# Windowed attention: the output transposed in PE's transpose mode into bf16 PSUM, copied by VectorE and kept by window

## Chip, cores, metric

One core of one Trainium2 chip. The metric is the device time of one execution in microseconds (us), median of two to seven runs of a kernel. The runs of the kernel before went from 5329 to 5375 us over the chips of this study, so each variant is judged against runs of the kernel before of the same call. All runs quoted here are of the state "fast".

## The reference, cut to what matters

```python
x0 = x + depthwise_conv3x3(x)                 # x: 1 x 511 x 511 x 192, bf16
h  = layernorm(x0)                            # over the 192 channels
hw = windows(h)                               # 7 x 7 windows: 5329 windows of 49 tokens
q, k, v = split(hw @ w_qkv)                   # 4 heads of 48
out = softmax(q k^T * 48**-0.5) v
return x0 + unwindow(out @ w_o)
```

## The kernel before

Windows are worked in 42 blocks of 128. A block has 16 steps, one for each chunk of 8 windows (392 tokens). The stages of several chunks overlap: in iteration g, A makes Q, K and V of chunk g, B the scores and the exponential of chunk g-1, D the weighted sum and its normalisation of chunk g-2, and E transposes the output of chunk g-3 into `OT`. Once a block there also run: the projection of the previous block (iteration 3), the convolution of the next block (iterations 7 to 10), the layer-norm statistics of the next block (iterations 11 to 15), with two "inverse roots" (1/std for 28 and then 21 tokens, each a chain of 15 small VectorE operations), and, at the start of the next block, the transposes of the normalised input (`hT`).

```python
PS = _Rot([psum.tile([128, 1024], F32, name=f"ps{i}") for i in range(4)])   # four PSUM buffers, in turn
OT = big.tile([128, 2, S * BLK], BF, name="OT")                            # S = 49 tokens, BLK = 128 windows
...
def build_D(blk, g):                       # diagonal matrices of 1/std: the transposes normalise as well
    nc.gpsimd.tensor_tensor(out=D[:], in0=ident_broadcast, in1=rstd[:, s0 : s0 + NDG]_broadcast, op=ALU.mult)
...
def transposes(blk):                       # 7 groups of 7 tokens, two halves of the channels each
    matmul(ps, lhsT=xc[:, s0 + ss, kt * KT : (kt + 1) * KT], rhs=D[:, ss, :])
    if kt == 0 or g % 2 == 0: nc.scalar.copy(out=hT..., in_=ps)
    else:                     nc.vector.tensor_copy(out=hT..., in_=ps)     # 3 of 14
...
def proj(blk):
    matmul(ps, lhsT=OT[0:KT, kt, (s0 + ss) * BLK : (s0 + ss + 1) * BLK], rhs=Wo[kt][0:KT, :])
...
def stage_E(g):
    for kt in range(2):
        for jj in range(4):
            nc.tensor.matmul(
                ps[0:KT, kt * 512 + jj * 2 * S : kt * 512 + (jj + 1) * 2 * S],
                lhsT=o_[:, jj, kt * KT : (kt + 1) * KT], rhs=idv, start=True, stop=True)
    nc.scalar.copy(
        out=OT[0:KT].rearrange("p k (s w) -> p k s w", w=BLK)[:, :, :, ck * CH : (ck + 1) * CH],
        in_=two_bank(ps, TOK)[0:KT].rearrange("p k (w s) -> p k s w", s=S))
...
if ck >= cend:                             # iterations 11 to 15
    stats_part(nb, sa, sb)                 # 10 rows of bn_stats on VectorE
    if sa < 28 <= sb:                      # the first inverse root, 28 rows
        stats_fin(nb, 0, 28);  build_D of groups 0 to 3   (GpSimd)
    if ck == NCH - 1:                      # the second inverse root, 21 rows
        stats_fin(nb, 28, 49); build_D of groups 4 to 6
```

`dve_help` decides who copies the second half of Q, K and V: VectorE in iterations 0 to 10, ScalarE in 11 to 15. A scheduler orders the instructions of each engine, so the written order is not quite the built one. The code above is shortened; "..." marks cuts, and names such as `ident_broadcast` stand for longer access patterns.

## Time and profile before

Median 5343.16 us (2 runs, 5342.79 to 5343.53). Mean length of the steps of a block in the profiled run, from the first QK matmul of one chunk to that of the next, in us:

| step | what lies in it | us |
|---|---|---|
| 0, 1 | plain | 4.80, 4.80 |
| 2 | projection | 14.34 |
| 3 to 5 | plain | 4.70, 4.78, 4.80 |
| 6, 7 | plain, then convolution and its wait for a load | 4.77, 20.11 |
| 8 to 10 | convolution and its end, granted clock 0.53 to 0.63 | 11.46, 7.32, 6.00 |
| 11 to 14 | statistics | 4.82, 4.73, 5.13, 4.99 |
| 15 | second inverse root, D, transposes | 15.87 |

The sum is 123.4 us a block. This is the group of the transposes (L346) in the kernel before: count, busy us, mean ns of one, then PE's idle time before them in us and what ended it; it will be compared later:

```profile
L346 PE MATMUL ps<-D,XC 128*96 128x128 bf16 x4116 | 338.4, 240 | 164.5 <-DVE hT L357 77.6 <-POOL D L327 35.8 <-ACT hT L355 26.2
```

In the whole run the transposes waited 36 us for GpSimd's diagonal matrices D (L327), and 78 us for VectorE's copies of earlier transposes (hT, L357), which in this kernel stand behind the second inverse root in VectorE's queue.

### The profile page before, as it was taken

The numbers are of one execution on the slowest core, as the hardware profiler recorded it, in microseconds if no ns is written. First come the engines' busy times: TensorE is split into PE (matmuls) and PEld (weight loads), VectorE is DVE, ScalarE is ACT, GpSimd is POOL, SyncE is SP. The second block draws the span as 40 slices with busy tenths as digits, with TensorE's granted clock in tenths as the row PEclk, the third lists the DMA queues.
The fourth block names the chain that finished last, engine by engine and source line by source line (L and its number), as shares of the span: only waits on it lengthen the run. The fifth ranks groups of instructions, "written<-read, shape, count | busy, mean of one in ns | idle before, by whom it ended". The sixth has DMA issues, their size and how long they took to land.

```text
span 5337.2 us, 148265 instructions
## 1 busy us (share of the span) xinstructions
PE 4490.1 (84%) x65427; PEld 3661.5 (69%) x65427; DVE 3816.7 (72%) x6912; ACT 2744.5 (51%) x3385; POOL 758.0 (14%) x833
## 2 busy tenths in 40 slices
PE   2788888888888888888988888888888888888887
PEld 1666676667776676677776777767666776677776
DVE  6776777767776777777677777777777777767776
ACT  1554555545555555555555455555555555545555
POOL 1111111111111111111111111111111111111120
PEclk9887888887778887888788877788888888877888
DMA  6554445554455555554455544455555445544431
GB/s 67 51 75 70 68 71 80 82 73 68 68 68 70 71 72 74 71 74 71 68 73 91 75 68 68 68 72 72 74 72 72 73 70 78 85 74 67 68 48 32
DMA packets 512613, 375.27 MB, mean 70 GB/s; under 512 B 453129, under 2 KB 453321, under 8 KB 511958
## 3 DMA queue, kind: packets, MB, share of 16 engines
q1 hardware_dynamic: 480918, 265.08, 38.1%
q0 software_dynamic: 30592, 100.32, 10.6%
q8 instruction: 514, 8.42, 0.7%
q14 instruction: 141, 1.16, 0.1%
q10 hardware_dynamic: 448, 0.30, 0.0%
HBM read 265.31 MB, written 100.27 MB: 68 GB/s over the span
## 4 chain that ended last, share of the span: by engine, by line
PE 44%; DVE 16%; ACT 14%; DMA 12%; SPq 9%; issue 4%; POOL 1%; DVEq 0%; ACTq 0%; POOLq 0%
PE ps L412 12%; PE ps L282 8%; SPq L396 7%; DMA out_dram<-XC 7%; PE ps L369 6%; DMA XC<-in_x_dram 5%; PE ps L453 5%; PE ps L532 4%; DVE kT L424 4%; ACT hT L355 4%; DVE Qb L422 3%; PE ps L431 2%; DVE XC L284 2%; PE ps L560 2%; ACT kT L426 2%
## 5 line engine op out<-in xcount | busy, mean ns | idle before, releaser
L412 PE MATMUL ps<-hT,Wqk 96*128 96x392 bf16 x5336 | 1233.5, 380 | 76.7 <-DVE XC L284 62.2
L478 ACT ACTIVATE PT<-ps 128x784 bf16<-128x784 f32 x667 | 552.7, 829 | 1095.3 <-PE ps L453 1080.3
L421 ACT CAST Qb<-ps 64x784 bf16<-64x784 f32 x667 | 555.3, 833 | 657.5 <-PE ps L412 655.7
L412 PEld LDWEIGHTS <-Wqk 96*128 96x128 bf16 x5336 | 529.4, 108 | 486.1 <-issue 252.5
L284 DVE TENSOR_TENSOR XC<-ps,XC 128x980 bf16<-128x980 f32 x378 | 437.9, 1176 | 503.0 <-PE ps L282 247.2
L282 PE MATMUL ps<-T,XP 81*128 81x49 bf16 x8064 | 744.0, 264 | 55.5 <-DMA XP<-in_x_dram 55.5
L567 ACT CAST OT<-ps 96x784 bf16<-96x784 f32 x667 | 541.0, 811 | 456.0 <-PE ps L560 452.4
L282 PEld LDWEIGHTS <-XP 81*128 81x128 bf16 x8064 | 733.9, 220 | 57.6 <-issue 55.5
L431 PE MATMUL ps<-Wv,hT 96*128 96x192 bf16 x5336 | 663.5, 277 | 16.4 <-DVE On L544 9.0
L532 PE MATMUL ps<-V,PT 49*64 49x49 bf16 x21344 | 542.5, 195 | 159.1 <-DVE Qb L422 81.2
L431 PEld LDWEIGHTS <-hT 96*128 96x128 bf16 x5336 | 548.8, 111 | 180.0 <-issue 91.6
L544 DVE TENSOR_TENSOR On<-ps,rs 128x768 bf16<-128x768 f32 x667 | 634.6, 951 | 16.0
L532 PEld LDWEIGHTS <-PT 49*64 49x64 bf16 x21344 | 466.2, 116 | 260.4 <-issue 217.7
L327 POOL TENSOR_TENSOR D<-ident,rstd 128x896 bf16<-128x896 bf16 x294 | 486.2, 1681 | 1074.8 <-DVE rstd L320 1053.3
L424 DVE CAST kT<-ps 128x784 bf16<-128x784 f32 x462 | 450.0, 974 | 219.2 <-PE ps L412 209.1
L304 DVE BATCH_NORM_STATS2 bnst<-XC 128x6 f32<-128x192 bf16 x2058 | 600.5, 343 | 0.2
L453 PE MATMUL ps<-Qb,kT 128*64 128x98 bf16 x10672 | 408.0, 225 | 180.7 <-DVE Qb L422 132.2
L422 DVE CAST Qb<-ps 64x784 bf16<-64x784 f32 x462 | 451.6, 978 | 110.6 <-ACT Qb L421 100.1
L355 ACT CAST hT<-ps 96x896 bf16<-96x896 f32 x462 | 452.4, 1109 | 135.9 <-PE ps L346 134.9
L560 PE MATMUL ps<-ident,On 128*96 128x98 bf16 x5336 | 412.1, 226 | 114.4 <-DVE kT L424 110.9
L453 PEld LDWEIGHTS <-kT 128*64 128x64 bf16 x10672 | 341.5, 121 | 231.5 <-issue 131.7
L108 POOL DMA_DIRECT2D XC<-in_x_dram x386 | 216.0, 560 | 1865.9 <-DVE rs L543 996.3
(73 smaller groups left out, 4396.2 us busy)
## 6 DMA issues: line engine op xcount, KB each, us to landing
XC<-in_x_dram POOLq DMA_DIRECT2D x277, 294.0 KB, 7.5
out_dram<-XC SPq DMA_DIRECT2D x277, 294.0 KB
XP<-in_x_dram SPq DMA_DIRECT2D x210, 246.4 KB
XP<-in_x_dram SPq DMA_DIRECT2D x68, 243.0 KB
XC<-in_x_dram POOLq DMA_DIRECT2D x37, 165.4 KB, 7.1
out_dram<-XC SPq DMA_DIRECT2D x37, 165.4 KB
XP<-in_x_dram SPq DMA_DIRECT2D x22, 216.0 KB
XP<-in_x_dram SPq DMA_DIRECT2D x18, 212.6 KB
```

The source lines that it names most:

```text
L282: nc.tensor.matmul(ps[:, col : col + S], lhsT=XP[0:KP, :, c], rhs=T[0:KP, c, :], start=True, stop=True)
L304: nc.vector.bn_stats(out=bnst[:, s, :], in_=xc[:, s, :])
L355: nc.scalar.copy(out=hv[0:KT, kt, :, s0 : s0 + NDG], in_=src)
L412: nc.tensor.matmul(ps[:, ab * 512 : ab * 512 + TOK], lhsT=Wqk[kt][0:KT, which * 2 + ab, :], rhs=hT[0:KT, kt, ck * CH : (ck + 1) * CH, 0:S] ...
L421: nc.scalar.copy(out=dst[0:64, :, :, 0, :], in_=src[0:64])
L422: (nc.vector.tensor_copy if dve_help else nc.scalar.copy)(out=dst[64:128, :, :, 1, :], in_=src[64:128])
L424: nc.vector.tensor_copy(out=dst[:, :, 0:TOK], in_=two_bank(ps, TOK))
L431: nc.tensor.matmul(ps[:, col : col + C], lhsT=hT[0:KT, kt, ck * CH + 2 * jj : ck * CH + 2 * jj + 2, :].rearrange("p w s -> p (w s)"), rhs= ...
L453: nc.tensor.matmul(ps[64 * wp : 64 * wp + 64, col : col + 2 * S], lhsT=k_[:, ab, w * S : w * S + 64], rhs=q_[:, ab, w, :, :].rearrange("p ...
L478: nc.scalar.activation(out=pt[:, 0 : 16 * S].rearrange("p (b n) -> p b n", b=2), in_=two_bank(ps, 8 * S), func=ACTF.Exp, scale=scale,)
L532: nc.tensor.matmul(ps[64 * wp : 64 * wp + 64, col : col + S], lhsT=pt[64 * wp : 64 * wp + S, pc_ : pc_ + 64], rhs=v_[64 * wp : 64 * wp + S ...
L544: nc.vector.tensor_tensor(out=o_[:].rearrange("p (b j) (h d) -> p b (j h) d", b=2, d=DH), in0=ov[:, :, :, 0:DH], in1=r_[:].rearrange("p (b ...
```

## The change

Intent: free ScalarE, which empties PSUM three to six times a step, of one copy; let the transposes write bf16 so that VectorE's copy gets shorter; and keep the output window by window, so that this copy's rows are written one after another. The price is that the projection's weights are then read with a step of 49 elements.

```diff
-        OT = big.tile([128, 2, S * BLK], BF, name="OT")
+        OT = big.tile([128, 2, BLK * S], BF, name="OT")
@@ proj
-                            lhsT=OT[0:KT, kt, (s0 + ss) * BLK : (s0 + ss + 1) * BLK],
+                            lhsT=OT[0:KT, kt, :].rearrange("p (w s) -> p s w", s=S)[:, s0 + ss, :],
@@ stage_E
+            pb = ps[:].bitcast(BF)
...
-                        ps[0:KT, kt * 512 + jj * 2 * S : kt * 512 + (jj + 1) * 2 * S],
+                        pb[0:KT, kt * 1024 + jj * 128 : kt * 1024 + (jj + 1) * 128],
                         lhsT=o_[:, jj, kt * KT : (kt + 1) * KT],
-                        rhs=idv,
+                        rhs=ident[:],
+                        is_transpose=True,
...
-            nc.scalar.copy(
-                out=OT[0:KT].rearrange("p k (s w) -> p k s w", w=BLK)[:, :, :, ck * CH : (ck + 1) * CH],
-                in_=two_bank(ps, TOK)[0:KT].rearrange("p k (w s) -> p k s w", s=S),
+            nc.vector.tensor_copy(
+                out=OT[0:KT, :, ck * TOK : (ck + 1) * TOK].rearrange("p k (w s) -> p k w s", s=S),
+                in_=pb.rearrange("p (k n) -> p k n", k=2)[0:KT, :, 0 : CH * 64].rearrange("p k (w s) -> p k w s", s=64)[:, :, :, 0:S],
             )
```

## The prediction

> **What bounds the kernel now.** I read the shares of the engines first. No engine is full, so the shares only say where to look.
>
> ```profile
> PE 4490.1 (84%) x65427; PEld 3661.5 (69%) x65427; DVE 3816.7 (72%) x6912; ACT 2744.5 (51%) x3385; POOL 758.0 (14%) x833
> ```
>
> ACT, which the change relieves, is the least loaded of the three compute engines, and DVE, which takes the work, is 1.4 times as busy. Next I cut one block of 16 steps (a step is one chunk of 8 windows; there are 42 blocks) out of the middle of the run at the first QK matmul of chosen steps, and asked for the busy time of each engine in five stretches: the projection of the previous block; four plain steps; the convolution; the steps with the layer-norm statistics; the last step with the transposes of the next block. Columns: us, then busy us of PE, weight loads, DVE, ACT, POOL, then the granted clock.
>
> ```profile
> 2659.57:2674.05 14.48, 14.05 (x201) 13.01 (x197) 10.45 (x13) 6.90 (x10) 0.00 (x0) 1.00 0.01 3
> 2674.05:2693.06 19.01, 15.37 (x292) 11.86 (x290) 15.84 (x19) 10.37 (x14) 3.74 (x7) 1.00 0.91 192
> 2693.06:2732.26 39.20, 35.06 (x415) 29.43 (x410) 23.34 (x26) 7.32 (x10) 1.34 (x3) 0.56 0.21 32
> 2732.26:2755.33 23.07, 19.36 (x363) 14.60 (x363) 21.22 (x76) 19.92 (x27) 2.67 (x6) 1.00 0.71 73
> 2755.33:2771.60 16.27, 12.29 (x175) 10.50 (x173) 11.32 (x26) 14.88 (x18) 9.90 (x7) 0.90 0.75 72
> ```
>
> The projection is PE's (14.05 of 14.48). In the statistics DVE has only 1.85 of 23.07 us free. The transposes look like ACT's (14.88 of 16.27). The convolution runs at a clock of 0.56. Then the timeline of the plain step and of the last step:
>
> ```profile
> 2657.44 0.98 DVE L422 CAST Qb<-ps 64x784 bf16<-64x784 f32 x1
> 2658.45 0.96 DVE L438 CAST V<-ps 128x768 bf16<-128x768 f32 x1
> 2659.57 1.53 PE L412 MATMUL ps<-hT,Wqk 96*128 96x392 bf16 x8
> 2659.68 0.26 DVE L543 RECIPROCAL rs<-ps 128x16 f32<-128x16 f32 x1 [0.27 <-PE ps L532]
> 2659.97 0.96 DVE L544 TENSOR_TENSOR On<-ps,rs 128x768 bf16<-128x768 f32 x1
> 2661.21 0.98 DVE L424 CAST kT<-ps 128x784 bf16<-128x784 f32 x1 [0.28 <-PE ps L412]
> ...
> 2763.05 4.97 POOL L327 TENSOR_TENSOR D<-ident,rstd 128x896 bf16<-128x896 bf16 x3 [2.78 <-DVE rstd L320]
> 2764.02 5.16 PE L346 MATMUL ps<-D,XC 128*96 128x128 bf16 x56 [2.27 <-DVE hT L357]
> ```
>
> The plain step is a loop: V's copy frees the PSUM buffer, QK's matmuls follow, then the copies of K, Q and V: 4.77 us from QK to QK. DVE is free in it only for 0.27 + 0.28 us. In the last step the transposes wait for the diagonal matrices D, those wait on POOL, and POOL waits for the last operation of the inverse root on DVE. So ACT's 14.88 us is busy work behind a chain that DVE starts. Last, the convolution's first evacuation waits for data:
>
> ```profile
> DVE XC L284 <- DMA XC<-in_x_dram: 215.9, 34, 10.5
> ```
>
> That is 6.4 us in each of 34 blocks: from the projection through store and load to the convolution runs a DMA chain, beside the plain steps.
>
> [...] the convolution's weights, 192 elements apart, take 220 ns a load where contiguous ones take 98. [...]
>
> ```profile
> L282 PEld LDWEIGHTS <-XP 81*128 81x128 bf16 x8064 | 733.9, 220 | 57.6 <-issue 55.5
> L369 PEld LDWEIGHTS <-OT 96*128 96x128 bf16 x4116 | 360.4, 98 | 27.6 <-issue 26.4 <-ACT OT L567 1.1
> L567 ACT CAST OT<-ps 96x784 bf16<-96x784 f32 x667 | 541.0, 811 | 456.0 <-PE ps L560 452.4
> ```
>
> **The change part by part.**
>
> ACT loses 667 copies x 811 ns = 541 us. Where is that on the path? In the plain steps ACT is half idle: nothing. In the statistics steps it looks like something, as ACT has 19.92 of 23.07. But without the copy Q's first half still cannot be read before QK's matmuls give it, and those come after the transposes of the same step on PE; I follow K's copy, scores, transposes, QK, the two Q copies and K's copy round and get 4.5 us against 4.6 now. So ACT's relief is worth about 0.1 us a step, and PE's longer transposes take it back.
>
> DVE gains 667 copies. [...] The built program of the changed kernel shows where they stand. In the plain step: after V's copy, ahead of the reciprocal. There V, copy, reciprocal, On need 0.03 + 0.57 + 0.03 + 0.29 + 0.96 + 0.03 = 1.91 us before K's copy, which now starts 1.80 after V's end: +0.11 a step. Of the some 6 such steps of a block, those between projection and convolution lie beside the DMA chain and are free; 2 count: 42 x 2 x 0.11 = 9 us.
>
> In the statistics steps: the scheduler also moves the rows, 10 in each of the first steps where there were 11, so the 28 rows that the first inverse root needs are ready a step's end later. From the fourth reciprocal (2750.3 by today's clock) I add 0.2 + 0.35 + 0.95 + 0.2 + 0.6 and ten pairs of one small operation and one row of 0.36: the first inverse root ends near 2755.8, against 2753.6 today. Then the fifth reciprocal, copy, On and nine rows (0.2 + 0.9 + 0.95 + 2.45) end near 2760.4, and the second inverse root follows with two of the hT copies (1.1 each) now in between, its first two operations held up by POOL's first four D as today (1.4 and 1.7 us): it ends near 2766 to 2768, against 2762.97. POOL's three D (4.97), the last transposes and the last copies hang on it rigidly. I take +3.8 us a block, x 41 = 156 us; 1.5 to 5.5 us is what my reading allows.
>
> PE's transposes stream 128 columns where they had 98. Today's spacing at full clock is (520 - 207)/7 = 45 ns for 98 columns (8 in 0.52 us); the hT transposes, 128 columns with weights of the same shape, go at 55 (7 in 0.55 us, of which 0.22 is the last). If PE mode keeps that, +10 ns x 8 a chunk, which counts only where PE bounds: in the convolution's three or four steps at half clock, where it is some 0.2 us each: 42 x 0.6 = 25 us.
>
> The projection's 4116 weight loads now step by 49 elements. The convolution's strided loads go every 90 ns (80 in 7.30 us); the projection's matmuls are 82 apart. If loads overlap the streams as now, 90 replaces 82 at most: 98 x 6 to 8 ns x 42 = 25 to 33 us, on PE's own stretch. I take 25.
>
> Sum: 5343 + 156 + 9 + 25 + 25 = 5558 us.
>
> **The rivals.** (a) Relief of ACT wins: the statistics and transposes drop by up to a copy a step, 6 x 0.8 x 41 = 197 us, to 5150. For it: ACT's 14.88 of 16.27. Against: D and the wait on the inverse root above. (b) [...] each copy costs 0.40 more; the two plain steps +34 us, the statistics +2 us a block = 82 us: 5670. [...] (c) A strided load does not hide under the stream: 90 + 20 to 80 ns a matmul, up to +280 us, to 5800. Against: in the convolution the streams are already under the loads. (d) [...] the clock falls in the plain steps as in the convolution (0.56): steps of 6.6 us in place of 4.8, over +500 us. [...] (e) The DVE delay is swallowed by other slack, as DVE is free 1.85 us in the statistics: then only some +60 to 100 us remain, within 2%.
>
> **Range and chances.** (e) is the main way to land within 2%, and needs the statistics stretch to lose under 1.2 us a block: 0.2. (b), (c), (d) all push up, so the range reaches further up: 5400 to 5740. Faster needs (a), against DVE's order: 0.03. Slower: 0.77.
>
> **What would show it.** DVE's OT copy at about 574 ns and DVE near 4200 us busy; plain steps of 4.9 us; the projection stretch 0.6 us longer; POOL's last three D of a block 3 to 5 us later after the convolution; the granted clock still 1.00 in the plain steps. I am wrong if the last D come no later, if the plain step shortens, or if strided loads cost far more than 90 ns.

The sum came to 5343 + 156 + 9 + 25 + 25 = 5558 us. The 574 ns for VectorE's bf16 copy enters the sums behind the 9 and the 156 as 0.57 and 0.6 us, and the 0.40 of rival (b) is the 974 ns of K's fp32 copy less it. No run before the change showed it, so read it there as an assumption of mine; the changed kernel's copy then took 560 ns (373.5 us in all), the fp32 copy of run 2 963.

## The result, and the profile after

Median 5525.51 us (2 runs, 5517.59 to 5533.42): slower, ratio 1.0336 with a 95% interval of 1.0295 to 1.0377. A ratio is the mean time of one kernel's fast runs over that of the other's of the same rounds, so it is not quite the ratio of the medians that I quote.

The shares of the engines of the changed kernel:

```profile
PE 4639.7 (84%) x65427; PEld 3773.8 (68%) x65427; DVE 4092.8 (74%) x7579; ACT 2257.2 (41%) x2718; POOL 758.0 (14%) x833
```

ACT lost 487 us of busy time, DVE gained 276, PE 150. The five stretches of a block from the middle of the run, cut at the same steps as in the prediction (us; busy us of PE, weight loads, DVE, ACT, POOL; granted clock; DMA share; GB/s):

```profile
2740.19:2754.78 14.59, 14.27 (x200) 13.20 (x196) 10.76 (x14) 6.99 (x10) 0.00 (x0) 1.00 0.01 2
2754.78:2774.17 19.39, 16.11 (x292) 12.22 (x291) 17.91 (x25) 6.68 (x9) 3.94 (x7) 1.00 0.91 191
2774.17:2813.17 39.00, 35.50 (x409) 29.79 (x408) 24.40 (x29) 4.95 (x6) 1.14 (x2) 0.56 0.23 31
2813.17:2836.43 23.26, 19.61 (x363) 15.00 (x363) 21.50 (x72) 17.08 (x22) 1.00 (x4) 1.00 0.71 74
2836.43:2856.03 19.60, 12.82 (x173) 11.07 (x172) 12.55 (x35) 14.60 (x17) 11.57 (x7) 0.83 0.75 69
```

Four stretches changed by less than 0.4 us. The last grew from 16.27 to 19.60. ACT does about the same amount of work there as before, 14.60 us, in a longer stretch: it waits. Selected lines from the timeline of that last stretch of the changed kernel (start us, us, engine, line, operation, in brackets the idle time before and what ended it):

```profile
2836.73 6.61 POOL L327 TENSOR_TENSOR D<-ident,rstd 128x896 bf16<-128x896 bf16 x4 [22.13 <-DVE rstd L320]
2836.93 0.50 DVE L569 COPY OT<-ps 96x784 bf16<-96x784 bf16 x1
2838.22 2.42 DVE L304 BATCH_NORM_STATS2 bnst<-XC 128x6 f32<-128x192 bf16 x9
2841.67 1.72 DVE L311 TENSOR_TENSOR tmp<-bnst 128x21 f32<-128x21 f32 x1
2843.73 1.08 DVE L357 CAST hT<-ps 96x896 bf16<-96x896 f32 x1
2845.89 1.08 DVE L357 CAST hT<-ps 96x896 bf16<-96x896 f32 x1
2847.79 4.97 POOL L327 TENSOR_TENSOR D<-ident,rstd 128x896 bf16<-128x896 bf16 x3 [4.45 <-DVE rstd L320]
2849.52 4.94 PE L346 MATMUL ps<-D,XC 128*96 128x128 bf16 x42 [4.10 <-POOL D L327]
```

The first four D begin 23.56 us after the stretch of statistics began (2813.17), where it was 21.40 before (2753.66 less 2732.26); the last three 34.62 us after, where it was 30.79. PE's transposes now wait for D, as their group says for the whole run:

```profile
L346 PE MATMUL ps<-D,XC 128*96 128x128 bf16 x4116 | 383.6, 257 | 285.4 <-POOL D L327 234.6 <-ACT hT L355 22.5 <-DVE hT L357 19.3
```

The wait for D grew by 199 us, but PE's idle time before the transposes by 121 only: two of the three hT copies now stand inside the second inverse root, so that less time is spent waiting for those.

Over all blocks, the steps' means changed like this (us a block): steps 0 and 1 -0.12; step 2 +0.10; steps 3 to 5 -0.01; 6 and 7 +0.31; 8 to 10 +0.32; 11 to 14 +0.42; 15 +3.67. The sum is 4.69, which times 41 to 42 blocks is the 194 us by which the two profiled spans differ. So nearly four fifths of the loss is in one step of sixteen. These are profiles of one execution each; differences of 0.1 to 0.4 us in steps 7 to 14 also occur between runs that change nothing there (run 4 has +0.25 in step 7).

### The profile page after: what moved, and what is told of

The parts are those of the page before. It is cut to its first block, busy times and chain, and to the rows that moved or that the text cites. A ratio compares the mean times of both kernels' runs of the same rounds, so it can differ in the third digit from the quotient of the medians.

```text
span 5531.4 us, 148053 instructions
## 1 busy us (share of the span) xinstructions
PE 4639.7 (84%) x65427; PEld 3773.8 (68%) x65427; DVE 4092.8 (74%) x7579; ACT 2257.2 (41%) x2718; POOL 758.0 (14%) x833
## 5 line engine op out<-in xcount | busy, mean ns | idle before, releaser
L412 PE MATMUL ps<-hT,Wqk 96*128 96x392 bf16 x5336 | 1249.0, 383 | 70.2 <-DVE XC L284 48.8
L412 PEld LDWEIGHTS <-Wqk 96*128 96x128 bf16 x5336 | 542.3, 109 | 484.9 <-issue 259.7
L346 PE MATMUL ps<-D,XC 128*96 128x128 bf16 x4116 | 383.6, 257 | 285.4 <-POOL D L327 234.6
L346 PEld LDWEIGHTS <-XC 128*96 128x96 bf16 x4116 | 346.5, 153 | 328.9 <-issue 264.2
L561 PE MATMUL ps<-ident,On 128*96 128x128 bf16 x5336 | 487.3, 243 | 95.5 <-DVE kT L424 91.8
L561 PEld LDWEIGHTS <-On 128*96 128x96 bf16 x5336 | 412.0, 139 | 152.6 <-issue 125.8
```

Source lines behind the costliest of these rows:

```text
L346: nc.tensor.matmul(ps[0:KT, ss * 128 : (ss + 1) * 128], lhsT=xc[:, s0 + ss, kt * KT : (kt + 1) * KT], rhs=D[:, ss, :], start=True, stop=True,)
L412: nc.tensor.matmul(ps[:, ab * 512 : ab * 512 + TOK], lhsT=Wqk[kt][0:KT, which * 2 + ab, :], rhs=hT[0:KT, kt, ck * CH : (ck + 1) * CH, 0:S] ...
L561: nc.tensor.matmul(pb[0:KT, kt * 1024 + jj * 128 : kt * 1024 + (jj + 1) * 128], lhsT=o_[:, jj, kt * KT : (kt + 1) * KT], rhs=ident[:], is_ ...
```

## The experiments

The theory: VectorE's copies, with the orders that come with them, delay the two inverse roots, GpSimd's D follow, and the transposes of the last step wait. The rivals: PE's transpose mode, the strided weights, or VectorE's time wherever it stands. To read the runs I took from each trace, in the mean over blocks 1 to 39, when the first and the fifth D begin after the QK of step 10: 23.62 and 33.10 us before, 26.08 and 37.51 in the changed kernel. From the fifth D to the end of step 15 it is 8.47 us before and 8.08 in the changed kernel, so the whole loss of these steps lies before the fifth D: 2.46 us of it before the first D, and 1.96 between the first and the fifth, where two hT copies of 1.08 us now stand. So the lower granted clock of step 15 (0.82, it was 0.91) costs nothing after the fifth D; what that of step 11 (0.83, it was 0.93) costs before it was not separated.

**1. ScalarE copies instead (changed kernel, one thing undone).**

```diff
-            nc.vector.tensor_copy(
+            nc.scalar.copy(
                 out=OT[0:KT, :, ck * TOK : (ck + 1) * TOK].rearrange("p k (w s) -> p k w s", s=S),
```

> The changed kernel with one thing undone: ScalarE instead of VectorE copies the bf16 transposes. Theory (the VectorE queue in front of the inverse root is the cost): the inverse root ends where it did before the change, POOL's last three D come at 30.8 us after the block's statistics begin, not 34.6, and the time is 5343 plus only what PE's longer transposes cost, 5345 to 5385. Rival (PE-mode transposes or strided weights cost most of it): 5450 or more whoever copies. ScalarE's copy of bf16 PSUM about 0.81 us.

Measured 5362.77 us, ratio 1.0024 (0.9981 to 1.0067). First D at 23.56, fifth at 32.98. The loss is gone, and in this build no hT copy stands inside the second inverse root; what PE mode and the layout cost together is not told apart from zero. The copy itself, in the groups of this run (mean ns of one after the comma):

```profile
L569 ACT COPY OT<-ps 96x784 bf16<-96x784 bf16 x667 | 540.4, 810 | 506.5 <-PE ps L561 485.8
```

ScalarE takes 810 ns for bf16 where it took 811 for fp32.

**2. VectorE copies, nothing else (kernel before, one thing done).**

```diff
-            nc.scalar.copy(
+            nc.vector.tensor_copy(
                 out=OT[0:KT].rearrange("p k (s w) -> p k s w", w=BLK)[:, :, :, ck * CH : (ck + 1) * CH],
```

> The kernel before with one thing changed: VectorE makes the attention output's copy, still fp32 and with the old layout. Theory: 784 fp32 elements cost VectorE about 0.97 us against 0.56, and five copies of a block lie ahead of the second inverse root, so some 2 us a block more than the change: 5560 to 5680. Rival (the loss comes from PE mode or the layout): 5343 to 5400.

Measured 5730.89 us, ratio 1.0700 (1.0633 to 1.0767): the expected direction, and more than expected. First D at 29.32, fifth at 41.05. One copy, in the groups of this run, beside that of the changed kernel:

```profile
L567 DVE CAST OT<-ps 96x784 bf16<-96x784 f32 x667 | 642.3, 963 | 138.2 <-PE ps L560 123.6
```

```profile
L569 DVE COPY OT<-ps 96x784 bf16<-96x784 bf16 x667 | 373.5, 560 | 52.2 <-PE ps L561 47.6 <-PE ps L282 2.9 <-ACT PT L478 0.6
```

So the bf16 part of the change is a gain on its own terms: it makes VectorE's copy 0.40 us shorter and with the rest of the change halves the loss. What I had not counted: with 963 ns the other steps grow too (step 2 by 1.19 us, step 6 by 0.91, steps 10 to 14 by 3.5). As in the changed kernel, two hT copies stand inside the second root here.

**3. Split by step (changed kernel).**

```diff
-        def stage_E(g):
+        def stage_E(g, on_act=False):
...
-            nc.vector.tensor_copy(
+            (nc.scalar.copy if on_act else nc.vector.tensor_copy)(
...
-                stage_E(g - LE)
+                stage_E(g - LE, on_act=(fast and ck >= 11))
```

> The changed kernel, but ScalarE copies in the five steps with statistics (steps 11 to 15 of a block) and VectorE in the others. Theory: the last-step loss of 3.7 us a block goes, about 150 us: 5355 to 5400. Rival (the loss is spread over all steps, or is a matter of the clock): the gain is in proportion, 5 of 16 copies of 182 us, so about 5465.

Measured 5421.00 us, ratio 1.0122 (1.0074 to 1.0170), a little above the 5355 to 5400 of the theory and clearly below the 5465 of the rival. Five of sixteen copies moved, 31% of them, and some 60% of the loss went. It is not all: first D at 24.30, fifth at 34.84, so 1.7 us of delay stay. The order of this build shows one reason that I had not foreseen: the scheduler put one hT copy inside the second inverse root here as well, and moved the rows of the statistics. The times tell them apart in part: from the first to the fifth D it is 10.55 us where it was 9.48, so the one hT copy makes 1.07 of the 1.74. The other 0.68 lies before the first D, and how it divides between the moved rows and the copies in the convolution steps was not separated.

**4. The layout alone (kernel before).**

```diff
-                            lhsT=OT[0:KT, kt, (s0 + ss) * BLK : (s0 + ss + 1) * BLK],
+                            lhsT=OT[0:KT, kt, :].rearrange("p (w s) -> p s w", s=S)[:, s0 + ss, :],
...
-                out=OT[0:KT].rearrange("p k (s w) -> p k s w", w=BLK)[:, :, :, ck * CH : (ck + 1) * CH],
-                in_=two_bank(ps, TOK)[0:KT].rearrange("p k (w s) -> p k s w", s=S),
+                out=OT[0:KT, :, ck * TOK : (ck + 1) * TOK],
+                in_=two_bank(ps, TOK)[0:KT],
```

> The kernel before with the layout alone: the copies stay fp32 and on ScalarE, the output is kept by window, so the projection's weight loads step by 49 elements. Theory: a load takes 141 ns in place of 98 but hides under the 192-column stream, matmuls stay 83 ns apart, and the time stays within 0.5% of 5343. Rival of my prediction: up to 8 ns a matmul, 5370. ScalarE's copy with rows written one after another may be a little shorter than 811 ns.

Measured 5345.54 us, ratio 0.9985 (0.9942 to 1.0029). The groups of this run for the projection's weight loads:

```profile
L369 PEld LDWEIGHTS <-OT 96*128 96x128 bf16 x4116 | 409.7, 142 | 22.9 <-issue 21.8 <-ACT OT L567 1.0
```

A load takes 142 ns where it took 98, and it is hidden: in this run's trace, as in the changed kernel's, the starts of the projection's matmuls (those that add the input included) are on average 83.6 ns apart, 83.5 before. ScalarE's copy took 809 ns, as with strided rows.

**5. All hT copies on ScalarE (changed kernel).**

```diff
-                    if kt == 0 or g % 2 == 0:
+                    if fast or kt == 0 or g % 2 == 0:
                         nc.scalar.copy(out=hv[0:KT, kt, :, s0 : s0 + NDG], in_=src)
```

> The changed kernel, with ScalarE making the three hT copies of a block that VectorE makes. In the trace of the changed kernel two of them, 1.08 us each, stand inside the second inverse root. Theory: without them the fifth D of a block comes about 2 us earlier (35.4 us after the QK of step 10 instead of 37.5), of which most reaches the end: 5525 less 41 x 1 to 2 us, 5440 to 5490. Rival (ScalarE with 14 copies then bounds the last step): no gain, 5510 to 5560.

Measured 5494.87 us, ratio 1.0293 (1.0259 to 1.0327), runs of the kernel before at 5343.61. The fifth D came 2.5 us earlier (35.03), as expected, and from the first D to the fifth it is 9.40 us again, as before the change, so the two hT copies do stand in the chain. But against the changed kernel the time fell by only some 23 us by the ratios, 31 by the medians, less than the 35 to 85 expected. As the two kernels were not run in the same call and the intervals of their ratios overlap, even that gain is not clear of noise. In the profiles step 15 gained 1.0 us and step 0 gave 0.46 back: after the fifth D the block now took 9.08 us in place of 8.08, and PE's transposes waited 43 us for ScalarE's hT copies in place of 22. So ScalarE, with 14 hT copies, seems to be the next limit. The rival of this run was half right.

**6 and 7. The same dummy work in two places (kernel before).** A sum over 384 elements of the output, thrown away; five a block, in iterations 3 to 7 or 11 to 15.

```diff
+            if pad:
+                nc.vector.tensor_reduce(out=junk[:], in_=o_[:, 0:2, :].rearrange("p j c -> p (j c)"), op=ALU.add, axis=AX.X)
...
-                stage_E(g - LE)
+                stage_E(g - LE, pad=(fast and 3 <= ck <= 7))        # run 6
+                stage_E(g - LE, pad=(fast and ck >= 11))            # run 7
```

> The kernel before, with a dummy VectorE operation of about 0.5 us (a sum over 384 elements of the attention output, thrown away) in steps 3 to 7 of each block, five a block, some 110 us of VectorE work in all. Theory (work there hides in the plain loop's gaps and beside the DMA chain): within 0.7% of the kernel before, 5343 to 5380. Rival (VectorE time counts wherever it stands): +110 us, 5450.

Measured 5398.99 us, ratio 1.0095 (1.0069 to 1.0121): more than expected, though only half of the VectorE time that was added.

> The kernel before with the same dummy operation, five a block, but in steps 11 to 15, ahead of and between the two inverse roots. Theory: it repeats the change's loss without PE mode, layout or bf16: the first D 2 us later, the fifth 3 to 4.5 us later, the time 5343 + 41 x 2.5 to 4 = 5445 to 5510. Rival (only the copies' PSUM buffers or PE matter): within 1% of before.

Measured 5499.06 us, ratio 1.0282 (1.0247 to 1.0317), as expected. The dummies in the groups of run 6 and of run 7:

```profile
L573 DVE TENSOR_REDUCE junk<-On 128x1 f32<-128x384 bf16 x210 | 116.1, 553 | 7.2
```

```profile
L573 DVE TENSOR_REDUCE junk<-On 128x1 f32<-128x384 bf16 x208 | 111.2, 534 | 0.1
```

The same 111 to 116 us of VectorE work cost 55 us in one place and 155 in the other. In run 7 the fifth D begins at 36.75 (+3.65) and step 15 is 3.17 us longer: the change's loss, without its transpose mode, layout or bf16. The dummies do not make all of it by their own time: in this build, too, the scheduler put two hT copies inside the second root, and 2.04 of the 3.65 us lie between the first and the fifth D. In run 6 no hT copy moved, and the fifth D stays at 33.13. Run 6 is not clean: as built, two of its five dummies stand ahead of the projection, and the scheduler swapped the K and Q copies in every other step; step 2 grew by 0.60 us and step 6 by 1.46, of which step 7, whose convolution waits for a load, gave 0.81 back.

**8. A try to beat both: Q's second half on ScalarE (kernel before).**

```diff
-                    (nc.vector.tensor_copy if dve_help else nc.scalar.copy)(out=dst[64:128, :, :, 1, :], in_=src[64:128])
+                    nc.scalar.copy(out=dst[64:128, :, :, 1, :], in_=src[64:128])
```

> A try to beat both: the kernel before, with the second half of Q copied by ScalarE in every step, which takes 0.98 us out of the VectorE loop of the plain steps (4.77 us) and puts 0.81 on ScalarE, idle there for 2.3 us. Theory: plain steps fall to about 4.0 us, but only the two before the projection and the projection's own step are on the path, as those after it lie beside the DMA chain: 42 x 1.5 to 2.5 us, 5240 to 5290. Rival (the plain steps are bounded by PE and its waits): 5330 to 5350.

Measured 5356.59 us (5317.31 to 5377.26), ratio 1.0032 (0.9997 to 1.0066): a miss. The profile is of the fastest of the four runs, the one of 5317 us. In it the plain steps did fall, from 4.78 to 4.25 us, but most of the gain was given back. Step 6 grew by 0.51 us, step 7 by 1.23, as the convolution's first evacuations waited longer for their load, and steps 11 to 13 by 0.93, at a mean granted clock of 0.77, 0.90 and 0.91 where it had been 0.95, 0.96 and 0.94. The wait, in the list of run 8, beside the 215.9 us in 34 blocks that the prediction quotes:

```profile
DVE XC L284 <- DMA XC<-in_x_dram: 280.8, 37, 11.3
```

**9. No wait for the second inverse root (run 5).**

```diff
-                in1=rstd[:, s0 : s0 + NDG].unsqueeze(2).to_broadcast([128, NDG, 128]),
+                in1=rstd[:, (g % 4) * NDG : (g % 4 + 1) * NDG].unsqueeze(2).to_broadcast([128, NDG, 128]),
...
-                        for gg in range(4):
+                        for gg in range(NG):
                             build_D(nb, gg)
...
-                            for gg in range(4, NG):
-                                build_D(nb, gg)
```

> A wrong result on purpose: the run with all hT copies on ScalarE, but the last three D of a block are built from the first inverse root's values right after the first four, so that no D waits for the second inverse root, which VectorE still computes. Instructions on PE and VectorE stand in the same order as in that run. Theory (the second root is what the last D, the transposes and the block's end wait for): the fifth D comes about 6.7 us after the first (it was 9.4), the last step 1.5 to 3 us shorter, 5495 less 41 x 1.5 to 3 = 5370 to 5435. Rival (the last step is bound by ScalarE's copies or by PE): 5480 to 5500.

Measured 5553.52 us, ratio 1.0374 (1.0318 to 1.0430): slower, against the expectation. (The comparison with the reference passed it although three groups of each block were scaled by other rows' values; it does not see this error.) The fifth D did come 6.6 us after the first, and PE waited 74 us for D in place of 168. But step 15 shrank by 0.3 us only, and step 0 grew by 1.1. Selected lines from the timeline of a last step of this run show two reasons:

```profile
2874.43 11.54 POOL L327 TENSOR_TENSOR D<-ident,rstd 128x896 bf16<-128x896 bf16 x7 [24.65 <-DVE rstd L320]
2879.37 1.72 DVE L311 TENSOR_TENSOR tmp<-bnst 128x21 f32<-128x21 f32 x1
2879.44 12.65 ACT L355 CAST hT<-ps 96x896 bf16<-96x896 f32 x13
2881.01 1.70 DVE L310 TENSOR_TENSOR tmp<-tmp 128x21 f32<-128x21 f32 x1
2882.64 1.72 DVE L312 TENSOR_SCALAR tmp<-tmp 128x21 f32<-128x21 f32 x1
2884.39 1.61 DVE L313 SCALAR_TENSOR_TENSOR tmp<-tmp,tmp 128x21 f32<-128x21 f32 x1
```

ScalarE copies without a gap for 12.65 us, so with hT on ScalarE it seems to bound the step, as the rival said (though the rival's time, 5480 to 5500, was missed as well). And while GpSimd makes D, operations of the inverse root that take 0.18 us otherwise take 1.6 to 1.7, each of the four in turn; one D takes about 1.65 there. A third thing is in the trace: the granted clock of step 0 was 0.63, where it was 0.92 in run 5 and 1.00 before. So the run moved other limits with the one that it was to test, and it does not show what the second root alone costs in the changed kernel.

## Why the prediction was right

Predicted 5558 us, 5400 to 5740; measured 5525.5. Step by step:

**The relief of ScalarE is worth nothing.** Nothing speaks against it. Its busy time fell from 2744.5 to 2257.2 us, and of the five stretches only the convolution got shorter, by 0.20 of 39 us. No run takes the copy off ScalarE without giving it to VectorE, so the worth of the relief alone was not measured; run 7, without the relief, loses about as much (1.0282) as the change (1.0336).

**VectorE's copy at 574 ns.** Right: 560. (VectorE's busy time is 4093 us where I said near 4200: the copies' own times add 373.5, but recorded operations overlap their neighbours, 71 us more than before, and busy time counts an overlap once; the other operations took 26 us less.) The runs show 560 ns, and not why. Run 2 shows the other case, 963 ns for fp32; VectorE's copies of K and Q, 784 fp32 elements too, take 974 and 978 in the kernel before.

**The inverse roots and the last step, +3.8 us a block, 156 us.** This is the term that carries the prediction, and it held: the first D 2.2 us later and the fifth 3.8 later in the block shown (in the mean 2.5 and 4.4), step 15 longer by 3.67 in the mean, some 150 us. Steps 11 to 14 added 0.42, some 17 us. Run 7 shows the mechanism, the moved hT copies included, without the rest of the change; run 1 shows its absence. That it costs more than the copies' own time (five copies, about 2.4 us at a spacing of 0.48) has a cause in the order: two hT copies came to stand inside the second root. Run 5, which takes them out, brings the fifth D 2.5 us earlier. Two slips did no harm. The terms listed for the first root add up to 2756.2, not 2755.8 (the block shown, whose first D came 2.16 us later, would give the latter). And the line on PE's transposes in the kernel before names VectorE's hT copy as what ended their wait of 2.27 us, not D, as the text has it; both stood behind the second root, on D's side through GpSimd. In the changed kernel it is D.

**Plain steps, +9 us.** Wrong in size: they became 0.06 us shorter before the projection, about -5 us in all. I added whole durations and gaps. The timeline of the changed kernel shows them overlapped:

```profile
2763.13 0.96 DVE L438 CAST V<-ps 128x768 bf16<-128x768 f32 x1
...
2764.01 0.56 DVE L569 COPY OT<-ps 96x784 bf16<-96x784 bf16 x1
2764.25 1.53 PE L412 MATMUL ps<-hT,Wqk 96*128 96x392 bf16 x8
2764.49 0.24 DVE L543 RECIPROCAL rs<-ps 128x16 f32<-128x16 f32 x1
2764.77 0.96 DVE L544 TENSOR_TENSOR On<-ps,rs 128x768 bf16<-128x768 f32 x1
2765.89 0.97 DVE L424 CAST kT<-ps 128x784 bf16<-128x784 f32 x1 [0.17 <-PE ps L412]
```

The copy is recorded as starting before V's has ended, and the reciprocal 0.48 us after the copy's start. So the copy fits into the 0.55 us that were free, and K's copy still waits 0.17 us for PE.

**PE's longer transposes, +25 us.** Too much: steps 8 to 10 grew by 0.32 us, 13 us in all, and as run 4, without these transposes, has +0.19 there, part of that may be noise. The spacing is as worked out: by the starts in the traces of the changed kernel and of the kernel before, the median at full clock is 56 ns for 128 columns and 45 for 98 (at a granted clock of 0.5, 107 and 81). The hT transposes, plain matmuls of 128 columns, follow each other every 56 ns too. One transpose took 243 ns in the mean, 219 in the median.

**Strided weights, +25 us.** Wrong: the projection's step grew by 0.10 us, 4 us in all (in run 4 it did not grow). I took the convolution's strided pace of 90 ns for every stride. The loads at a step of 49 hide under the stream: 142 ns a load against 98, the matmuls 83.6 ns apart (run 4). The convolution's loads, 192 elements apart, took 220 ns in the kernel before and 212 in the changed one, and its matmuls came about every 89 ns, at full and at half clock alike.

**Not foreseen:** 13 us in steps 6 and 7, where QK's matmuls now wait for the copy (12.4 us in 41 waits), and VectorE's queue before the convolution is longer.

These misses are small and partly cancel: -5 + 4 + 13 where 9 + 25 + 25 was said, and 13 not foreseen.

**The rivals.** Relief of ScalarE, (a): no. A VectorE copy dearer by 0.40 us, (b): no, 560 ns. Loads not hidden, (c): no (its sum was off too: 80 ns on each of 4116 loads are 329 us, not 280). A falling clock, (d): no, the granted clock is 1.00 in the plain stretch, and run 1, with the same transposes, has 0.824 over the whole run, as the kernel before; as plain matmuls stand around the transposes in every step, what they do to the clock alone was not tested. Slack that swallows the delay, (e): no.

**Left open:** how the 0.68 us by which the split run's first D is late divide between the moved statistics rows and the copies in the convolution steps; how much of run 7's loss would stay if the hT copies kept their place; and what the second root alone costs in the changed kernel, as run 9 moved other limits with it. No variant here beats the kernel before; the layout alone (run 4) is not told apart from it.

## What to carry to other kernels

Before work is moved to an engine, ask what waits behind it in that engine's queue: the same 0.11 ms of VectorE work cost 55 us in one place and 155 in another, because in the second a short chain of small operations stood behind it on which another engine and then the transposes depended, and because the scheduler put two more copies into that chain. A busy engine in a stretch (ScalarE at 14.88 of 16.27 us) can be waiting work behind a chain that starts elsewhere; relieve the start of the chain, not the busy engine. And read the built order: those two copies made nearly half of the delay of the fifth D, and the diff does not show them.
